# Phase 1 with x also stored by features, its mean subtracted by accumulating DMAs and no transposes of x

## The chip, the cores and the metric

The kernel runs on one core of a Trainium2 chip. The metric is the device time of one execution in microseconds; a time is the median of three runs.

## The reference

One transformer block over x of 2048 tokens by 640 features, all in float32:

```python
mod = (_silu(c) @ w_mod).reshape(c.shape[0], 6, 1, -1)
sa, ca, ga, sb, cb, gb = ...
h = _layernorm(x) * (1 + ca) + sa
x = x + ga * _A_ref(h, A_wqkv, A_w_phi, A_wo)
h = _layernorm(x) * (1 + cb) + sb
x = x + gb * _B_ref(h, B_w1, B_b1, B_w2, B_b2)
```

`_A_ref` projects h to q, k and v in 32 heads of 20 features, maps q and k of each head by a 20 x 20 matrix and two softmaxes (of the value and of its negative), sums the outer products of mapped k and v over all tokens, and divides what q reads from that sum by a normaliser. `_B_ref` is two dense layers with a squared ReLU between them. This case is about the first `_layernorm` and the three projections behind it.

## The kernel before

The 2048 tokens are 16 tiles of 128, taken in pairs j = 0 to 7. Phase 1 makes, for each pair, the normalised and modulated features `hT` with the features on the partitions: five chunks d of 128 features by 256 tokens, each as a rounded high part and a low remainder. TensorE multiplies them with the folded weights for k, v and q of each tile. A projection (`proj`, L402) is 30 matmuls, into two PSUM banks of 384 and 256 columns; there are four such banks (`pj`), so a third projection in a row needs the banks of the first.

How a pair's features are made (before):
- `load_x` (L221) loads 256 tokens by 640 features, tokens on the partitions, into one of two slots.
- `ln_parts` (L333) has three parts: ScalarE sums each row (L339) and GpSimd makes the negative mean (L340); ScalarE sums the squares of the centred row (L344) and GpSimd takes the root (L345, L346) and the product (L347); ScalarE scales and shifts the rows in place (L350).
- `t1` (L388) has TensorE turn chunks of 128 x 128 by the identity matrix into PSUM (`t_in`, L363, tile `ta`), and `t_out` has ScalarE apply the modulation (L374) and round to the high part (L375), and VectorE subtract for the low part (L89, `lo`).

The loop of phase 1 (L718) goes over tiles t = 2 to 13, with t = 2j and 2j + 1 for pair j. For each it has the k projection and its evacuation by ScalarE, the v projection, in even tiles the products of k and v of the two tiles before (`do_kv`, L450, tile `kvp`), the softmax of k (`spread` L433 on VectorE, `exps` L440 on ScalarE, `k_norm` L444 on VectorE), the q projection (tiles below 12; for 12 to 15 it comes later) and the softmax of q (`q_chain`, L471). The statistics of pair j + 1 are taken in the even tile of pair j, its first two chunks are turned at the end of that tile, the other three in the odd tile. For pair 7 the statistics already start in tile 10 and 11 and the chunks are spread over tiles 12 and 13. Between, the vectors of the modulation are accumulated by VectorE (`mod_mac`, L321) from rows of `w_mod` that SyncE loads into five slots, and `spread_row` (L329) writes the gate, a column of 5 elements on each of 128 partitions, to DRAM (L330) and fetches it back as a row spread over all partitions (L331), in tile 7's side work.

In this loop the order of TensorE is written out by hand. The orders of VectorE, ScalarE, GpSimd and SyncE are set by a scheduler with a time model of its own; each engine then works its list strictly in that order, and a waiting instruction holds up all behind it. SyncE issues nearly all DMAs; GpSimd issues one here, since it alone can accumulate or change types.

Of the kernel before, what the change touches and what calls it, by code (L numbers as in the profile page):

```python
# [21 lines left out]
NT = S // P  # L22
NC = D // P
# [9 lines left out]
EPS = 1e-5  # L33
POSTPONED = 4
WARM = 9
KEPT = NT - POSTPONED
W2_AT = 48
PLAIN = 2
DEALT = range(NT // 2)
# [13 lines left out]
def kernel(  # L53
    ctx: ExitStack,
    tc: tile.TileContext,
    x: bass.AP,
    wk5: bass.AP,
    wk1: bass.AP,
    wq5: bass.AP,
# [13 lines left out]
    nc = tc.nc  # L73
# [24 lines left out]
    dram = ctx.enter_context(tc.tile_pool(name="dram", bufs=1, space=bass.MemoryType.DRAM))  # L98
# [40 lines left out]
    def tp(name):  # L139
        return psA.tile([P, 512], F32, tag="tp", name=name)  # L140
# [6 lines left out]
    ET_ = mybir.EngineType  # L147
# [19 lines left out]
    mhalf = const.tile([P, 2], F32, name="mhalf")  # L167
# [3 lines left out]
    cols_a = const.tile([P, 10], F32, name="cols_a")  # L171
# [38 lines left out]
    raw, WM, RV, XB = {}, {}, {}, {}  # L210
# [8 lines left out]
                nc.sync.dma_start(raw[nm][2][:40, 1], w1)  # L219

    def load_x(j):  # L221
        XB[j] = tok2(f"x{j % 2}", f"xb{j}")
        nc.sync.dma_start(XB[j], x[256 * j : 256 * j + 256].rearrange("(i p) d -> p i d", p=P))

    def load_wm(d):
        WM[d] = flat(tok2(("k", "k", "q0", "q1", "w")[d], f"wm_{d}"))
# [106 lines left out]
    def ln_parts(xt, nm, spare=None):  # L333
        sm = small([P, 2], "sm", f"sm{nm}")
        sq = small([P, 2], "sq", f"sq{nm}")
        nb = small([P, 2], "nb", f"nb{nm}")
        for i in range(2):
            same = spare[i] if spare else xt[:, i] if nm[0] == "a" else row("s3", f"same{nm}_{i}")
            nc.scalar.activation(same, xt[:, i], AF.Identity, accum_out=sm[:, i : i + 1])  # L339
        nc.gpsimd.tensor_scalar(sm, sm, -1.0 / D, None, op0=ALU.mult)  # L340
        yield
        for i in range(2):
            junk = spare[i] if spare else row("s3", f"junk{nm}_{i}")
            nc.scalar.activation(junk, xt[:, i], AF.Square, bias=sm[:, i : i + 1], accum_out=sq[:, i : i + 1])  # L344
        nc.gpsimd.tensor_scalar(sq, sq, 1.0 / D, EPS, op0=ALU.mult, op1=ALU.add)  # L345
        nc.gpsimd.tensor_tensor(sq, sq, mhalf, op=ALU.pow)  # L346
# [4 lines left out]
        yield  # L351

    def layer_norm(xt, nm, spare=None):
        for _ in ln_parts(xt, nm, spare):
            pass
# [23 lines left out]
    HT, PK, EK, EQ, PQ = {}, {}, {}, {}, {}  # L379
# [3 lines left out]
    def newest(engine):  # L383
        return next(i for i in reversed(nc.cur_bb.bb.instructions) if i.engine == engine)

    DONE = []

    def t1(j, *ds, more=None):  # L388
        if 0 in ds:
            HT[j] = ht(f"hT{j}", j)  # L390
        p = tp(f"ta{j}_{ds[0]}")
# [72 lines left out]
    def q_out(t, p):  # L464
        if t < KEPT:
            PQ[t] = row("s2", f"q{t}")
# [4 lines left out]
    def q_chain(t, whole=True):  # L471
        if t < KEPT:
            EQ[t] = tok2(f"q{t % 2}", f"eq{t}")
# [53 lines left out]
    def wo_weights(*gs):  # L527
# [189 lines left out]
    pe.__enter__()  # L717
    for t in range(2, NT - 2):  # L718
        j, i = divmod(t, 2)
        if i == 0 and j < NT // 2 - 2:  # L720
            load_x(j + 2)
        PK[t] = row("s2", f"k{t}")
        to_sb(proj("k", t), PK[t])
        if t == NT - 4:
            t1(j + 1, 0, 1)
        norm = j + 1 if i == 0 and t < NT - 4 else j + 2 if t == NT - 5 else None
        if norm:
            if not i:
                parts = ln_parts(XB[norm], f"a{norm}")
# [12 lines left out]
        spread(PK[t], EK[t], f"k{t}")  # L742
        exps(EK[t])
        if norm and not i:
            next(parts)
        if i and t < NT - 4:
            t1(j + 1, 2, 3)
        with tc.issue_after(newest(ET_.DVE)):
            k_norm(EK[t], t)
        if t < NT - POSTPONED:  # L750
            do_q(t, (1, 3, lambda: t1(j + 1, 4, more=LAST_COL.get(t))) if i else None)
            if norm and i:
                with tc.issue_after(newest(ET_.Activation)), tc.issue_after(DONE[0]):
                    next(parts)
# [7 lines left out]
        if t == NT - 6:  # L762
            parts = ln_parts(XB[j + 2], f"a{j + 2}")
            with tc.issue_after(newest(ET_.Activation)):
                next(parts)
        SIDE[t]()
    pe.__exit__(None, None, None)
    behind.close()
# [96 lines left out]
    def load_e(t):  # L865
        if t >= KEPT:
            if t < NT:
# [320 lines left out]
    for j in range(NB):  # L1188
        nxt = j + 1 < NB
        b, c = 2 * j + 5, 2 * j + 6  # L1190
# [56 lines left out]
        if j == 7:  # L1247
            t2(0, 4)
            p = tp("gbt")[:NC, :P]
# [463 lines left out]
    by_hand.__exit__(None, None, None)  # L1713


_INS = ["x", "wk5", "wk1", "wq5", "wq1", "wv", "bd", "c", "w_ss", "w_mod", "wo", "w1", "b1", "w2", "b2"]


# [53 lines left out]
```

## Time and profile before

| | |
|---|---|
| time, median of 3 runs | 756.91 us (756.39 to 757.07) |
| span of the profiled execution | 754.9 us |
| TensorE busy | 749.6 us (99%) |
| VectorE busy | 607.5 us (80%) |
| ScalarE busy | 458.8 us (61%) |
| GpSimd busy | 170.4 us (23%) |
| share of TensorE in the chain that ended last | 86% |
| phase 1's loop, pairs 1 to 6 | 52.33 to 224.10 us |

The profiled execution is known by its span, from the first to the last instruction of the program; the runs' median is 2.0 us above it. In the profile's rows, PE is TensorE, PEld its weight loads, DVE VectorE, ACT ScalarE, POOL GpSimd and SP SyncE; a q behind a name means the engine's sequencer. L79 is the line of the helper that issues nearly all matmuls, so these are told apart by their tiles: pk, pv, pq for the three projections, kvp for the products of k and v. A row of a group gives the number of instructions, their busy time in us, the mean of one in ns, and the idle time of the engine just before them with what ended it. A row of a timeline gives the start and the length in us.

### The profile page before, as it was taken

The page shows a single profiled execution, that of the slowest core. Times are in us where ns is not written, and L with a number is a line of the kernel's source. Part 1 is how long each engine was busy: PE and PEld are TensorE (multiplying, and loading weights), DVE is VectorE, ACT ScalarE, POOL GpSimd, SP SyncE. Part 2 cuts the span into 40 slices and gives each one's busy share as a digit, 9 for nine tenths or more (in the row PEclk, how much of TensorE's full clock was granted, in tenths as well). Part 3 has the DMA queues.
Part 4 walks back from the last instruction along what each step waited for, and adds up shares of the span by engine and source line. Part 5 has one row for each costly group of instructions (what it writes and reads, how often), then busy time and mean ns, then how long its engine had stood idle before and what let it go on. Part 6 is the DMA issues. An engine that isn't in the chain of part 4 may idle for free.

```text
span 754.9 us, 15404 instructions
## 1 busy us (share of the span) xinstructions
PE 749.6 (99%) x5888; PEld 731.9 (97%) x5888; DVE 607.5 (80%) x1123; ACT 458.8 (61%) x1060; POOL 170.4 (23%) x365
## 2 busy tenths in 40 slices
PE   9999999999999999999999999999999999999998
PEld 9999999999999998998899999999999999999997
DVE  6598987988999899999755768787777776777766
ACT  5767666677863355556677757485574756647431
POOL 3001101011200237646303030132221313213110
PEclk9999999999999999999999999999999999999999
DMA  9811431342432264664777475897677767667461
GB/s 324 336 39 80 155 96 70 106 139 103 138 105 93 71 190 142 143 153 124 173 204 218 121 216 215 278 326 204 185 213 204 205 196 212 191 181 208 132 188 36
DMA packets 58931, 126.70 MB, mean 168 GB/s; under 512 B 7452, under 2 KB 16417, under 8 KB 58857
## 3 DMA queue, kind: packets, MB, share of 16 engines
q1 hardware_dynamic: 38706, 79.41, 32.1%
q0 software_dynamic: 17568, 41.00, 22.0%
q10 hardware_dynamic: 2583, 5.30, 1.9%
q8 instruction: 46, 0.75, 0.5%
q14 instruction: 28, 0.23, 0.1%
HBM read 100.94 MB, written 29.89 MB: 173 GB/s over the span
## 4 chain that ended last, share of the span: by engine, by line
PE 86%; DVE 11%; POOL 1%; issue 1%; ACT 0%; DVEq 0%; POOLq 0%
PE up L79 24%; PE acc L79 18%; PE pk L79 9%; PE pv L79 9%; PE pq L79 8%; PE acc3x L79 5%; PE pwo L79 3%; PE kvp L455 3%; DVE dn L883 3%; DVE scr L881 2%; DVE ezb L905 2%; PE foldk L281 1%; PE ta L363 1%; DVE ot L89 1%; POOL dn L889 1%; PE foldq L281 1%
## 5 line engine op out<-in xcount | busy, mean ns | idle before, releaser
L79 PE MATMUL up<-h,w 128*128 128x256 f32 x1640 | 204.4, 276 | 0.1
L79 PEld LDWEIGHTS up<-h,w 128*128 128x128 f32 x1640 | 196.4, 188 | 0.5 <-DVE h L89 0.3
L1321 ACT ACTIVATE ft<-up,b_t 128x256 f32<-128x256 f32 x104 | 48.9, 471 | 96.0 <-PE up L79 95.6
L79 PE MATMUL acc<-w,ra 128*128 128x384 f32 x452 | 97.5, 335 | 0.0
L79 PE MATMUL pwo<-wo,ot 128*128 128x256 f32 (+3 forms) x512 | 79.9, 311 | 0.4 <-DVE ot L89 0.4
L1322 DVE TENSOR_TENSOR ft<-ft 128x256 f32<-128x256 f32 x104 | 43.8, 421 | 43.0 <-ACT ft L1321 41.4
L79 PEld LDWEIGHTS pwo<-wo,ot 128*128 128x128 f32 (+1 forms) x512 | 74.3, 188 | 3.5 <-issue 2.7
L79 PE MATMUL pq<-wq,hT 128*128 128x384 f32 (+1 forms) x480 | 75.1, 311 | 0.0
L79 PEld LDWEIGHTS acc<-w,ra 128*128 128x128 f32 x452 | 72.7, 188 | 0.9 <-DVE ra L89 0.6
L79 PE MATMUL pk<-wk,hT 128*128 128x384 f32 (+1 forms) x480 | 72.7, 308 | 0.0
L79 PE MATMUL pv<-wv,hT 128*128 128x384 f32 (+1 forms) x480 | 71.6, 306 | 0.0
L79 PEld LDWEIGHTS pq<-wq,hT 128*128 128x128 f32 x480 | 71.0, 188 | 0.6 <-issue 0.2
L79 PEld LDWEIGHTS pk<-wk,hT 128*128 128x128 f32 x480 | 70.5, 188 | 0.4 <-issue 0.2
L79 PEld LDWEIGHTS pv<-wv,hT 128*128 128x128 f32 x480 | 70.0, 188 | 0.0
L89 DVE TENSOR_TENSOR ra<-ft,ra 128x384 fp32r<-128x384 f32 (+2 forms) x86 | 36.8, 449 | 32.7 <-ACT ra L1345 19.4
L1431 POOL DMA_DIRECT2D ring_a<-td_a x34 | 18.5, 544 | 117.1 <-PE acc L79 103.7
L1345 ACT ACTIVATE ra<-ft 128x384 fp32r<-128x384 f32 x48 | 25.2, 526 | 28.5 <-DVE ft L1322 22.4
L79 PE MATMUL acc3x<-w,ra 128*128 128x256 f32 x231 | 39.5, 278 | 0.0
L79 PEld LDWEIGHTS acc3x<-w,ra 128*128 128x128 f32 x231 | 37.2, 188 | 0.0
L1336 DVE TENSOR_TENSOR ft<-ft 128x128 f32<-128x128 f32 x136 | 33.4, 286 | 1.2
L446 DVE TENSOR_REDUCE sk<-ek 128x64 f32<-128x1280 f32 x16 | 23.7, 1483 | 12.4 <-ACT ek L441 10.8
L889 POOL TENSOR_TENSOR dn<-dn,rs_q 128x32 f32<-128x32 f32 x32 | 19.9, 622 | 59.0 <-DVE dn L883 58.7
(264 smaller groups left out, 1458.2 us busy)
## 6 DMA issues: line engine op xcount, KB each, us to landing
ring_c<-td_c POOLq DMA_DIRECT2D x34, 384.0 KB, 4.1
ring_a<-td_a POOLq DMA_DIRECT2D x34, 384.0 KB, 3.5
ring_b<-td_b POOLq DMA_DIRECT2D x34, 256.0 KB, 3.5
esp<-eq SPq DMA_DIRECT2D x12, 640.0 KB, 3.2
el<-esp SPq DMA_DIRECT2D x12, 640.0 KB, 4.4
rw<-in_w SPq DMA_DIRECT2D x23, 320.0 KB, 3.5
wm<-in_w_mod SPq DMA_DIRECT2D x20, 320.0 KB, 3.7
xb<-in_x SPq DMA_DIRECT2D x8, 640.0 KB, 4.0
```

The lines of the kernel that those rows point to most:

```text
L79: nc.tensor.matmul(o, a, b, start=first and i == 0, stop=last and i == len(terms) - 1, skip_group_check=skip,)
L89: (eng or nc.vector).tensor_tensor(out_lo, full, hi.bitcast(F32), op=ALU.subtract)
L281: nc.tensor.matmul(p[g // 3][:, (g % 3) * 120 : (g % 3) * 120 + n], r, bd_t[:120, g * 120 : g * 120 + n], start=True, stop=True,)
L446: nc.vector.tensor_reduce(s, heads(flat(e)), axis=AX.X, op=ALU.add)
L455: nc.tensor.matmul(kvp[g // 4][64 * c : 64 * c + 64, a : a + 2 * n].rearrange("p (s n) -> p s n", s=2), v[:, u], e[:, :, o : o + n], start ...
L883: nc.vector.tensor_reduce(dn.rearrange("p s h -> p (s h)"), heads(z), axis=AX.X, op=ALU.add)
L889: nc.gpsimd.tensor_tensor(dn[:, s], dn[:, s], rs[:, 1 - s], op=ALU.mult)
L1321: nc.scalar.activation(r, p, AF.Relu, bias=b1_t[:, f : f + 1])
L1322: nc.vector.tensor_tensor(r, r, r, op=ALU.mult)
L1336: nc.vector.tensor_tensor(t[:, o], t[:, a], t[:, b], op=op)
L1345: nc.scalar.activation(a[:, 0, :3], t[:, :3], AF.Copy)
L1431: nc.gpsimd.dma_start(RING[j, n, r], TD[n][r].bitcast(F32R))
```

## The change

The host stores x a second time as `x_t`: for each pair a block of 128 partitions by 5 chunks by 256 tokens, features on the partitions. From pair 2 on (TURNED = 2):

- `load_xt` loads that block into the slot `x1`; the block by tokens takes the slot `x0` alone, and is used for the statistics only.
- `row_parts` replaces `ln_parts`: the sums and the means as before, then `put_row` writes the negative means (two elements on each of 128 partitions) to DRAM as a row of 256, and `centre` has GpSimd issue two accumulating DMAs that add this row to every partition of the features' block. Then the squares, the root, a second `put_row`, and `get_row`, which fetches the row of factors spread over all partitions.
- `t1` has VectorE multiply the block by that row (new line 431), and `t_out` reads the product from SBUF in place of PSUM. TensorE turns no x from pair 2 on; it still turns the pieces of the modulation.
- All pairs follow one scheme: statistics of pair j + 1 in the even tile of pair j. That holds for pair 7 too, whose features are now made in pair 6 alone. `load_x` for pair j + 2 comes behind the statistics of pair j + 1.

```diff
+TURNED = 2
...
+    def put_row(j, k, col):
+        nc.sync.dma_start(LR[j][k].rearrange("(i p) -> p i", p=P), col)
+
+    def centre(j):
+        for a, b in ((0, 2), (2, NC)):
+            nc.gpsimd.dma_start(XT[j][:, a:b], LR[j][0][None, None, :].to_broadcast([P, b - a, 256]), accum_op=ALU.add)
+
+    def get_row(j):
+        RB[j] = row("s3", f"rb{j}")[:, :256]
+        nc.sync.dma_start(RB[j], LR[j][1][None, :].to_broadcast([P, 256]))
...
+    def row_parts(j):
...
+        for i in range(2):
+            nc.scalar.activation(xt[:, i], xt[:, i], AF.Identity, accum_out=sm[:, i : i + 1])
+        nc.gpsimd.tensor_scalar(sm, sm, -1.0 / D, None, op0=ALU.mult)
+        put_row(j, 0, sm)
+        centre(j)
+        yield
+        for i in range(2):
+            nc.scalar.activation(xt[:, i], xt[:, i], AF.Square, bias=sm[:, i : i + 1], accum_out=sq[:, i : i + 1])
...
+        nc.gpsimd.tensor_tensor(sq, sq, mhalf, op=ALU.pow)
+        put_row(j, 1, sq)
+        get_row(j)
+        yield
...
+        if j >= TURNED:
+            u = XT[j][:, ds[0] : ds[-1] + 1]
+            nc.vector.tensor_tensor(u, u, RB[j][:, None, :].to_broadcast([P, len(ds), 256]), op=ALU.mult)
...
+            for d in ds:
+                t_out(cols_a, HT[j], d, f"a{j}", XT[j][:, d], XT[j][:, d])
...
-        12: lambda: t1(NT // 2 - 1, 2, 3),
...
-        if i == 0 and j < NT // 2 - 2:
-            load_x(j + 2)
+        if i == 0:
+            load_xt(j + 1)
...
-        if norm and not i:
+        if i == 0:
             next(parts)
+            if j < NT // 2 - 2:
+                load_x(j + 2)
...
-        if i and t < NT - 4:
+        if i:
             t1(j + 1, 2, 3)
...
-        if i == 0 and t < NT - 4:
+        if i == 0:
             t1(j + 1, 0, 1)
```

VectorE's order in pair 2, before, behind the softmax's sums of k of tile 4: the two maxima of q (`mxq`), then the low parts of the first two chunks of the next pair (`hT`).

```order
L448 TENSOR_TENSOR ek_1263<-ek_1263,sk_1273 128x1280
L435 TENSOR_REDUCE mxq_1313<-q_1309 128x32
L436 TENSOR_REDUCE mxq_1313<-q_1309 128x32
L89 TENSOR_TENSOR hT_1322<-hfa_0_1328,hT_1322 128x256
L89 TENSOR_TENSOR hT_1322<-hfa_1_1332,hT_1322 128x256
L297 SCALAR_TENSOR_TENSOR wm_1_1336<-wm_1_1336,cs,wm_0_1152 128x640
L438 TENSOR_TENSOR eq_1312<-q_1309,mxq_1313 128x640 x2
```

The same place with the change; `xt` is the block by features, `rb` the fetched row of factors.

```order
L484 TENSOR_REDUCE mxq_1306<-q_1302 128x32
L485 TENSOR_REDUCE mxq_1306<-q_1302 128x32
L496 RECIPROCAL sk_1266<-sk_1266 128x64
L487 TENSOR_TENSOR eq_1305<-q_1302,mxq_1306 128x640
L431 TENSOR_TENSOR xt_1144<-xt_1144,rb_1254 128x512 x2
L431 TENSOR_TENSOR xt_1144<-xt_1144,rb_1254 128x256
L487 TENSOR_TENSOR eq_1305<-q_1302,mxq_1306 128x640
L497 TENSOR_TENSOR ek_1258<-ek_1258,sk_1266 128x1280
L484 TENSOR_REDUCE mxk_1401<-k_1329 128x32
L485 TENSOR_REDUCE mxk_1401<-k_1329 128x32
L91 TENSOR_TENSOR hT_1315<-xt_1144,hT_1315 128x256 x2
```

All five chunks are multiplied at one place, between the two halves of the softmax's differences of q (`eq`), and the low parts come behind the normalising of k and the maxima of the next tile's k.

SyncE's order at the start of pair 4, before: the load of x for a later pair, the gate's column and its fetch, the store of a tile of exponentials (`esp`).

```order
L223 DMA xb_1849<-in_x 128x2x640
L330 DMA gate_186<-gate_a 128x5x1
L331 DMA ga_b<-gate_186 128x640
L485 DMA esp_195<-eq_1834 128x1280
L316 DMA wm_4_2037<-in_w_mod 128x640
L496 DMA rwo_2191<-in_wo 60x640 x2
```

The same place with the change; `lr` are the two rows of statistics in DRAM.

```order
L231 DMA xt_1817<-in_x_t 128x1280
L350 DMA gate_186<-gate_a 128x5x1
L351 DMA ga_b<-gate_186 128x640
L235 DMA lr_0_1819<-sma_1856 128x2x1
L225 DMA xb_1936<-in_x 128x2x640
L534 DMA esp_195<-eq_1802 128x1280
L235 DMA lr_1_1820<-sqa_1857 128x2x1
L336 DMA wm_4_2003<-in_w_mod 128x640
L545 DMA rwo_2149<-in_wo 60x640 x2
L243 DMA rb_1934<-lr_1_1820 128x256
```

Both rows of statistics and the fetch of the factors stand behind the gate's column and its fetch.

GpSimd's order around the statistics of pair 3's features, with the change.

```order
L379 TENSOR_SCALAR sma_1183<-sma_1183 128x2
L239 DMA xt_1144<-lr_0_1146 128x2x256
L239 DMA xt_1144<-lr_0_1146 128x3x256
L385 TENSOR_SCALAR sqa_1184<-sqa_1184 128x2
L386 TENSOR_TENSOR sqa_1184<-sqa_1184,mhalf 128x2
```

The two accumulating DMAs, which wait for the first row in DRAM, stand ahead of the root that the second row needs.

More of the change, by code (lines that the diff above doesn't have):

```diff
@@ L56 @@
     x: bass.AP,
+    x_t: bass.AP,
     wk5: bass.AP,
@@ L221, in load_x, with load_xt @@
     def load_x(j):
-        XB[j] = tok2(f"x{j % 2}", f"xb{j}")
+        XB[j] = tok2(f"x{j % 2}" if j < TURNED else "x0", f"xb{j}")
         nc.sync.dma_start(XB[j], x[256 * j : 256 * j + 256].rearrange("(i p) d -> p i d", p=P))
+    XT, LR, RB = {}, {}, {}
+    def load_xt(j):
+        XT[j] = flat(tok2("x1", f"xt{j}")).rearrange("p (d n) -> p d n", d=NC)
+        nc.sync.dma_start(XT[j], x_t[j * P : (j + 1) * P].rearrange("p (d n) -> p d n", d=NC))
+        LR[j] = [dram.tile([256], F32, name=f"lr{j}_{k}") for k in range(2)]
+    def put_row(j, k, col):
[6 more added lines that the diff above has]
+        nc.sync.dma_start(RB[j], LR[j][1][None, :].to_broadcast([P, 256]))
     def load_wm(d):
@@ L351, in ln_parts @@
         yield
+    def row_parts(j):
+        xt = XB[j]
+        sm = small([P, 2], "sm", f"sma{j}")
+        sq = small([P, 2], "sq", f"sqa{j}")
+        for i in range(2):
[6 more added lines that the diff above has]
+            nc.scalar.activation(xt[:, i], xt[:, i], AF.Square, bias=sm[:, i : i + 1], accum_out=sq[:, i : i + 1])
+        nc.gpsimd.tensor_scalar(sq, sq, 1.0 / D, EPS, op0=ALU.mult, op1=ALU.add)
+        nc.gpsimd.tensor_tensor(sq, sq, mhalf, op=ALU.pow)
+        put_row(j, 1, sq)
+        get_row(j)
+        yield
     def layer_norm(xt, nm, spare=None):
@@ L719 @@
         j, i = divmod(t, 2)
-        if i == 0 and j < NT // 2 - 2:
-            load_x(j + 2)
+        if i == 0:
+            load_xt(j + 1)
         PK[t] = row("s2", f"k{t}")
         to_sb(proj("k", t), PK[t])
[L724 to L729, printed above, removed]
+        if i == 0:
+            parts = row_parts(j + 1)
             with tc.issue_after(newest(ET_.Activation)):
@@ L743 @@
         exps(EK[t])
-        if norm and not i:
-            next(parts)
-        if i and t < NT - 4:
+        if i:
             t1(j + 1, 2, 3)
@@ L759 @@
                 q_chain(t)
-        if i == 0 and t < NT - 4:
+        if i == 0:
             t1(j + 1, 0, 1)
[L762 to L765, printed above, removed]
         SIDE[t]()
```

12 lines of the change are left out of this document (8 added, 4 removed).

## The prediction

> **What bounds the kernel now.** I read the shares of the chain that ended last, then a table of stretches cut at the starts of the pairs of phase 1, then TensorE's timeline of one such pair.
>
> ```profile
> by line: PE up L79 24.5%; PE acc L79 18.0%; PE pk L79 9.2%; PE pv L79 9.1%; PE pq L79 7.8%; PE acc3x L79 5.0%; PE pwo L79 3.5%; PE kvp L455 2.6%; DVE dn L883 2.6%; DVE scr L881 2.5%; DVE ezb L905 2.2%; PE foldk L281 1.0%; PE ta L363 0.9%; D
> ```
> ```profile
> core 0: us, PE busy (x) PEld busy (x) DVE busy (x) ACT busy (x) POOL busy (x), PEclk, DMA share, GB/s
> 52.33:82.14 29.81, 29.81 (x237) 29.59 (x235) 26.84 (x34) 20.98 (x48) 2.31 (x6) 1.00 0.24 86
> 82.14:111.95 29.81, 29.81 (x236) 29.59 (x235) 26.82 (x35) 19.56 (x44) 2.84 (x4) 1.00 0.36 116
> 111.95:142.32 30.37, 30.37 (x241) 30.15 (x240) 26.18 (x35) 19.33 (x45) 2.83 (x4) 1.00 0.30 99
> 142.32:172.65 30.33, 30.33 (x242) 30.11 (x241) 26.88 (x34) 21.05 (x48) 2.88 (x6) 1.00 0.35 108
> 172.65:202.97 30.32, 30.32 (x242) 30.10 (x241) 27.69 (x35) 24.47 (x58) 7.07 (x11) 1.00 0.32 108
> 202.97:224.10 21.13, 21.13 (x176) 20.88 (x175) 20.53 (x30) 12.92 (x30) 0.00 (x0) 1.00 0.37 124
> ```
> ```profile
> 82.14 4.46 PE L79 MATMUL pk<-wk,hT 128*128 128x384 f32 x30
> 86.44 4.46 PE L79 MATMUL pv<-wv,hT 128*128 128x384 f32 x30
> 90.83 2.54 PE L455 MATMUL kvp<-ek,vt 128*64 128x120 f32 x44
> 93.30 4.64 PE L79 MATMUL pq<-wq,hT 128*128 128x384 f32 x30
> 97.78 0.60 PE L363 MATMUL ta<-ident,xb 128*128 128x128 f32 x4
> ```
>
> The rows of the table are pairs j = 1 to 6. TensorE is busy from end to end of each, at full clock, so what is removed from it there shortens the kernel, as long as nothing else becomes late. VectorE is the near rival: 26.8 of 29.8 us, and 20.5 of 21.1 in pair 6. Below, times within a pair count from its first key matmul (82.14 is 0 for pair 2).
>
> **What the change removes.** The 60 transposes of x (ta L363) hold 0.9% of the chain: 0.009 x 754.9 = 6.8 us, 1.1 per pair. A plain pair falls from 29.8 to about 28.7. ScalarE loses the two scalings L350, and has slack anyway.
>
> **What it adds on VectorE.** One multiplication of 1280 elements per pair, in three pieces.
>
> ```profile
> L448 DVE TENSOR_TENSOR ek<-ek,sk 128x1280 f32<-128x1280 f32 x10 | 14.8, 1485 | 0.1
> L446 DVE TENSOR_REDUCE sk<-ek 128x64 f32<-128x1280 f32 x10 | 14.9, 1485 | 11.1 <-ACT ek L441 10.6 <-ACT ek L442 0.2
> L438 DVE TENSOR_TENSOR eq<-q,mxq 128x640 f32<-128x640 f32 x22 | 17.0, 811 | 0.0
> L435 DVE TENSOR_REDUCE mxk<-k 128x32 f32<-128x640 f32 x10 | 8.1, 811 | 0.0
> L89 DVE TENSOR_TENSOR hT<-hfa,hT 128x256 fp32r<-128x256 f32 x24 | 9.3, 419 | 1.5 <-ACT hT L375 1.5
> ```
>
> By L448 that is 1.5 us, so VectorE has 28.3 us of work for a pair of 28.7: alone it would just fit, since the 10.6 us in which it waited for the exponentials of k mostly followed the two removed scalings. But it has no room left to wait.
>
> **What it adds as a wait.** The statistics now reach the features through DRAM: sums, a row of 256 means written in 4-byte pieces, the accumulating DMA, then the root, a second such row, and a broadcast fetch. In the order of the change GpSimd has the accumulating DMAs ahead of the root, so the two writes follow one another. VectorE stands in order behind the fetch. The nearest rows are these: sums of pair 2, GpSimd's small steps, the one column write of before and a row write, and small loads.
>
> ```profile
> 86.64 0.39 ACT L431 ACTIVATE k<-pk 128x256 f32<-128x256 f32 x1 [0.42 <-PE pk L79]
> 88.27 0.19 ACT L339 ACTIVATION_READ_ACCUMULATOR xb<-xb 128x1 f32 x1
> ```
> ```profile
> L346 POOL TENSOR_TENSOR sqa<-sqa,mhalf 128x2 f32<-128x2 f32 x6 | 5.5, 924 | 0.5
> L345 POOL TENSOR_SCALAR sqa<-sqa 128x2 f32<-128x2 f32 x6 | 2.5, 413 | 14.3 <-ACT junka L344 14.3
> L340 POOL TENSOR_SCALAR sma<-sma 128x2 f32<-128x2 f32 x6 | 1.8, 294 | 120.5 <-ACT xb L339 120.5
> L508 POOL DMA_DIRECT2D wo<-wo x1 | 0.8, 789 | 34.0 <-DVE wo L89 34.0
> ```
> ```profile
> 144.26 0.38 SPq L330 DMA_DIRECT2D gate<-gate_a  x1
> 154.62 0.34 SPq L331 DMA_DIRECT2D ga_b<-gate  x1
> ```
> ```profile
> 388.53 0.28 SPq L1252 DMA_DIRECT2D gate<-gate_r  x1
> 389.73 0.32 SPq L1253 DMA_DIRECT2D gb_b<-gate  x1
> ```
> ```profile
> rwo<-in_wo SPq DMA_DIRECT2D x10, 150.0 KB, 2.5
> ga_b<-gate SPq DMA_DIRECT2D x1, 320.0 KB, 3.9
> rawv<-in_wv SPq DMA_DIRECT2D x5, 320.0 KB, 11.5
> ```
>
> The fetch at 154.62 reads what the write at 144.26 puts down, and is SyncE's next DMA: the write of 640 single elements held the queue 10.4 us. Its twin, the same 2.5 KB as five rows of 512 bytes, let its fetch go after 1.2 us. So the price lies in the number of pieces. I take 1.2 as the part without pieces and scale the rest: W = 1.2 + 9.2 x 256/640 = 4.9 us for a row of 256. Ends: 1.2, and 10.4 if the price does not fall with the count.
>
> The Trainium skill ("DMA: Bandwidth & Descriptors", "Anatomy of one DMA") gives a DMA a fixed cost of about 2.0 us plus its bytes, which would make W 2.0. The 10.4 us of this trace do not agree with it for 2.5 KB, and I go by the trace; what W = 2.0 would do is the first rival.
>
> The chain of a plain pair: sums read at 88.27 + 0.19, so 6.3; L340 0.3 and the issue, 6.7; W, 11.6; two accumulating DMAs issued by GpSimd at 0.8 each (L508), 13.2; L345 and L346, 14.5; W, 19.5; the fetch of 128 KB at 2.5 us (nearest row 150 KB; 3.9 as upper end), 22.0. Before, VectorE would be at this place after the two maxima of q, when pq ends at 97.78 (15.6): some 17.5 to 19. So it waits 3 to 4.5 us per pair. The accumulating DMA of 640 KB is hidden if it lands within 8.8 us; 11.5 us, the slowest load above, would add 2.7. ScalarE too stands in order behind the multiplication, with the second half of the next tile's k to evacuate behind that; that has a few us of room.
>
> From the multiplication to the last hT subtraction VectorE has in pair 2: 1.5, one half of eq 0.8, ek 1.5, two maxima 1.6, five subtractions 2.1, one step for the modulation 0.9, two halves of ek 1.6, one sum of eq 1.5: 11.5, or 11.0 with the pipelined overlap of about 0.08 each that the timeline's starts show. So the last features are there at 33.0; the next pair's first projection needs them 2.0 us after its start (4.3 us x 384/640 for its first bank, x 12/15 matmuls), so it starts in effect at 31.0 instead of 29.8: +1.2. In pairs 1 and 3 fewer steps stand between (10.3, 10.5): +0.5 and, against 30.4, +0.2. Sum for three pairs: +1.9.
>
> **Pair 4, behind the gate.** Here SyncE's order has the gate column's write and fetch ahead of the first row. The gate's sum follows the late features, so the write goes at about 4.2, the fetch 10.4 later, and the row at 15.0 instead of 6.7. Statistics land at 30.3. ScalarE's evacuation of tile 9's k waits behind them, to about 34.5 (multiply 1.3, scalings and copies of four chunks); the q projection of tile 9 needs that PSUM bank, so TensorE, which would have been there at 24.3, stands 10 us; with pq 4.3 the pair ends at 38.8 against 30.3: +8.5. VectorE has then 12.7 us of delayed work until tile 9's keys are normalised, 13.1 into pair 5, where kvp wants them at 8.7: 4.4 of waiting, less the gain: +2.9.
>
> **Pair 6.** Before, its successor's features were prepared from tile 11 on; now all of it lies in the short pair 6. Features of pair 7 begin at 22.0; first chunk at 24.2, five chunks at ScalarE's pace by 27.5, so the key projection starts at 25.5 in effect against 21.1: +4.4, and 0.5 for tile 13's steps pushed behind.
>
> Sum: 1.9 + 8.5 + 2.9 + 4.9 = +18.2. The span is 754.9, and the median of the runs, 756.9, is 2.0 above it for what lies around; I forecast 756.9 + 18.2 = 775. Each 1 us in W moves up to 2 us in six pairs, 12 in all; with W at 6 and the fetch at 3.9, or the accumulation late by 2.7, it is 795 to 805.
>
> **Rivals.**
> (a) Small writes are cheap here (chance 0.17): W 1.2, by the row write. The fetch lands at 14.6, ahead of VectorE; all 6.8 us are gained. Pair 4 keeps the gate in front: row at 15.0, statistics at 22.9, the bank free at 27.1 instead of 24.3: some +2.4. 756.9 - 6.8 + 2.4 = 752.5. For it: 5 rows took 1.2 us. Against: the 10.4 us. The skill's fixed 2.0 us puts the fetch at 16.2 and gives the same 752.5.
> (b) The write's time does not fall with the count (0.08): W 10.4, chain 11 us longer in six pairs: 775 + 66 = 841.
> (c) W near 3 (0.13): the fetch lands at 18.2, about when VectorE comes; pairs 1 to 3 gain 3.5, pair 4 loses 4.5, pairs 5 and 6 1.6: 759.5. A little less W turns its sign: slower 0.08, same 0.03, faster 0.02.
> My own case (W 4 to 6) has 0.62.
>
> Slower: 0.62 + 0.08 + 0.08 = 0.78; same 0.03; faster 0.17 + 0.02 = 0.19, the bound being 0.2% (1.5 us), about what a measurement tells here. The range runs from (a), 752, to the upper end of my case, 805; outside it stay (b) and a tenth.
>
> **What would show it.** Right: the fetch of the first row issued some 5 us after its write; VectorE idle before L431 for 3 us and more, longest in pair 4; TensorE's first gaps in phase 1, at pq of tile 9, at kvp and at the first pk of pair 7. Wrong: second-row fetches issued within 2 us of their writes, no gap on TensorE, phase 1 shorter by 1.1 us a pair; or equal gaps of 11 us in every pair.

## The result and the profile after

| | before | change |
|---|---|---|
| time, median | 756.73 us (756.16 to 757.07, 5 runs) | 887.64 us (886.85 to 890.24, 5 runs) |
| span of the profiled execution | 754.9 us | 885.2 us |
| TensorE busy | 749.6 us (99%) | 764.1 us (86%) |
| clock granted to TensorE, mean of the span | 1.00 in phase 1 | 0.93, in phase 1 0.78 to 0.84 |

The ratio is 1.1743 (95% interval 1.1730 to 1.1756): slower by 131 us, where 775 us (752 to 805) was forecast. The sign was right, the size was not, and the range did not hold it.

The chain that ended last, by engine and by line, of the profile after. The entries `lr<-sqa`, `lr<-sma`, `xt<-lr` and `rb<-lr` are the new transfers:

```profile
PE 60%; DVE 13%; DMA 11%; issue 11%; ACT 3%; POOL 1%; SPq 0%; POOLq 0%; DVEq 0%; ACTq 0%
PE up L81 21%; PE acc L81 15%; PE pwo L81 5%; PE acc3x L81 4%; PE pq L81 4%; DMA lr<-sqa 4%; PE pk L81 4%; DMA lr<-sma 3%; DMA xt<-lr 2%; PE pv L81 2%; PE te L962 1%; DMA rb<-lr 1%; DVE ezb L942 1%; DVE dn L920 1%; DVE scr L918 1%
```

The table of stretches, cut at the first key matmul of pairs 1 to 6 and at the end of pair 6, as it was shown of before:

```profile
core 0: us, PE busy (x) PEld busy (x) DVE busy (x) ACT busy (x) POOL busy (x), PEclk, DMA share, GB/s
52.20:98.09 45.89, 30.58 (x227) 29.75 (x225) 22.86 (x30) 16.65 (x41) 4.41 (x7) 0.82 0.44 61
98.09:144.71 46.62, 32.99 (x224) 32.00 (x225) 27.09 (x37) 17.28 (x43) 3.78 (x5) 0.83 0.53 105
144.71:195.53 50.82, 32.84 (x229) 31.52 (x230) 28.92 (x39) 19.08 (x47) 4.28 (x5) 0.84 0.43 87
195.53:254.17 58.64, 33.10 (x231) 32.56 (x230) 30.20 (x42) 18.64 (x46) 4.92 (x7) 0.78 0.51 105
254.17:305.33 51.16, 31.86 (x231) 31.44 (x230) 27.46 (x38) 20.33 (x47) 5.43 (x8) 0.80 0.48 82
305.33:350.18 44.85, 21.93 (x166) 21.30 (x165) 23.50 (x31) 14.76 (x33) 3.71 (x5) 0.79 0.53 98
```

Every pair is longer, by 16 to 28 us: together 298.0 us against 171.8, which is 126 of the 130 us between the spans. TensorE, busy from end to end before, works 30.6 of the first 45.9 us, and at 0.82 of its clock. What it waits for in phase 1 (engine, tile, what ended the wait; total, times, longest):

```profile
PE pq L81 <- ACT k L480: 86.7, 5, 23.3
PE pk L81 <- ACT k L480: 17.5, 1, 17.5
PE kvp L504 <- DVE ek L497: 7.9, 3, 5.4
```

TensorE stands before the queries of the odd tile (in pair 6 before the first keys of pair 7) because ScalarE has not evacuated the keys, and ScalarE stands behind VectorE's multiplication. The next views follow that back in pair 1. ScalarE's part first: it waits 21.16 us for the multiplication, then scales two chunks (L412), then evacuates the keys (L480).

```profile
92.29 1.09 ACT L412 ACTIVATE xt<-xt,cols_a 128x256 f32<-128x256 f32 x2 [21.16 <-DVE xt L431]
93.29 0.36 ACT L480 ACTIVATE k<-pk 128x256 f32<-128x256 f32 x1
```

SyncE's queue, GpSimd and VectorE, each a start and a length:

```profile
58.84 0.38 SPq L235 DMA_DIRECT2D lr<-sma  x1
78.70 0.37 SPq L235 DMA_DIRECT2D lr<-sqa  x1
87.61 0.33 SPq L243 DMA_DIRECT2D rb<-lr  x1
```
```profile
69.22 1.43 POOL L239 DMA_DIRECT2D xt<-lr  x1 [9.84 <-DMA lr<-sma]
75.92 1.30 POOL L239 DMA_DIRECT2D xt<-lr  x1 [5.26 <-issue]
77.31 0.29 POOL L924 TENSOR_SCALAR dd<-dd 128x32 f32<-128x32 f32 x1
77.68 0.19 POOL L385 TENSOR_SCALAR sqa<-sqa 128x2 f32<-128x2 f32 x1
77.95 0.72 POOL L386 TENSOR_TENSOR sqa<-sqa,mhalf 128x2 f32<-128x2 f32 x1
```
```profile
91.57 1.63 DVE L431 TENSOR_TENSOR xt<-xt,rb 128x512 f32<-128x512 f32 x3 [21.56 <-issue]
```

The chain has the order that the prediction gave it; its links are longer. From the pair's start at 52.20, in us:

| link | predicted | measured |
|---|---|---|
| sums, L379, issue of the first row | 6.7 | 6.6 |
| first row of 256, to GpSimd's next instruction | 4.9 | 10.4 |
| two accumulating DMAs issued | 1.6 | 8.1 |
| to the issue of the second row | 1.3 | 1.4 |
| second row, to the issue of the fetch | 4.9 | 8.9 |
| fetch, to the multiplication | 2.5 | 4.0 |
| multiplication starts at | 22.0 | 39.4 |

Two rows show their wait as "issue", for which the profile names no semaphore. The multiplication's 21.56 us end when the fetch has landed, 3.9 us after its issue; both accumulating DMAs had landed by 83.3. The second accumulating DMA waits 5.26 us, and is issued at 75.92, just when the first has landed (75.66).

TensorE in the same pair; the third row is the start of pair 2:

```profile
76.44 2.76 PE L81 MATMUL pq<-wq,hT 128*128 128x384 f32 x15
93.70 3.57 PE L81 MATMUL pq<-wq,hT 128*128 128x256 f32 x15 [14.50 <-ACT k L480]
98.09 2.29 PE L81 MATMUL pk<-wk,hT 128*128 128x384 f32 x6 [0.81 <-ACT vt L475]
```

The last row's six matmuls take 2.29 us, 0.38 each; the fifteen of the first row, of the same width, took 0.18 each. The stretch around the gap shows why (the third number from the end is the granted clock, 0.50):

```profile
81.80:102.30 20.50, 7.78 (x28) 7.49 (x29) 10.73 (x18) 8.26 (x21) 0.00 (x0) 0.50 0.18 43
```

So the clock fell to half 2.6 us after the last matmul and came back 8.6 us after work had begun again, with short waits between. By the trace's clock records, the six long gaps differ in this: the fall came 2.6 to 5.3 us after the last matmul, the return 4.7 to 8.6 us after the first new one. In the six pairs TensorE is busy 183.3 us, where 171.8 less the 6.8 of transposes is 165.0: some 18.3 us, an estimate, are the price of matmuls at half clock. The Trainium skill ("TensorE: Matmul & The Clock Gate", "Part 1: The HAM clock gate") has the clock halve after an idle window of some 3.4 us and return after as long a busy one. The trace agrees with the half; the times scatter around that figure for the fall and lie above it for the return.

The other transfers also grew. Issues of phase 1's DMAs (KB each, median us to landing), first of before, then of after:

```profile
esp<-eq SPq DMA_DIRECT2D x12, 640.0 KB, 3.2
xb<-in_x SPq DMA_DIRECT2D x8, 640.0 KB, 4.0
```
```profile
esp<-eq SPq DMA_DIRECT2D x12, 640.0 KB, 10.7
xb<-in_x SPq DMA_DIRECT2D x8, 640.0 KB, 10.9
xt<-lr POOLq DMA_DIRECT2D x6, 384.0 KB, 8.4
xt<-lr POOLq DMA_DIRECT2D x6, 256.0 KB, 7.0
rb<-lr SPq DMA_DIRECT2D x6, 128.0 KB, 3.9
```

The medians of `esp` and `xb` in the change rest on few DMAs: the profile tells the landing of three of the twelve stores (11.2, 2.9 and 10.7 us) and of two of the loads (10.6 and 11.3). The store of 2.9 us was issued at 97.63, when no row was on its way. So it is the transfers beside a row that are slow, not all.

Theory after this: the rows of 4-byte pieces cost some 9 us whatever their count, and the accumulating DMAs hold GpSimd, so the multiplication starts 17 us late and everything behind it follows. Rivals: the accumulating DMAs are slow by themselves; VectorE has no room for the multiplications, so that the pairs would be long without any late statistics; ScalarE's order does it.

### The profile page after: what moved, and what is told of

Its sections match the earlier page's. It is cut to its first block, busy times and chain, and to the rows that moved or that the text cites. A ratio compares the mean times of both kernels' runs of the same rounds, so it can differ in the third digit from the quotient of the medians.

```text
span 885.2 us, 15380 instructions
## 1 busy us (share of the span) xinstructions
PE 764.1 (86%) x5828; PEld 742.7 (84%) x5828; DVE 615.8 (70%) x1141; ACT 448.3 (51%) x1048; POOL 179.3 (20%) x371
## 4 chain that ended last, share of the span: by engine, by line
PE 60%; DVE 13%; DMA 11%; issue 11%; ACT 3%; POOL 1%; SPq 0%; POOLq 0%; DVEq 0%; ACTq 0%
PE up L81 21%; PE acc L81 15%; PE pwo L81 5%; PE acc3x L81 4%; PE pq L81 4%; DMA lr<-sqa 4%; PE pk L81 4%; DMA lr<-sma 3%; DMA xt<-lr 2%; PE pv L81 2%; PE te L962 1%; DMA rb<-lr 1%; DVE ezb L942 1%; DVE dn L920 1%; DVE scr L918 1%
## 5 line engine op out<-in xcount | busy, mean ns | idle before, releaser
L81 PE MATMUL pq<-wq,hT 128*128 128x384 f32 (+1 forms) x480 | 84.4, 337 | 86.7 <-ACT k L480 86.7
L81 PEld LDWEIGHTS pq<-wq,hT 128*128 128x128 f32 x480 | 79.9, 211 | 88.7 <-ACT k L480 88.1
L431 DVE TENSOR_TENSOR xt<-xt,rb 128x512 f32<-128x512 f32 (+1 forms) x18 | 9.9, 599 | 135.4 <-DMA rb<-lr 68.3
L81 PE MATMUL pk<-wk,hT 128*128 128x384 f32 (+1 forms) x480 | 79.3, 325 | 19.5 <-ACT k L480 17.5
L81 PEld LDWEIGHTS pk<-wk,hT 128*128 128x128 f32 x480 | 76.6, 201 | 21.5 <-ACT k L480 17.7
L412 ACT ACTIVATE xt<-xt,cols_a 128x256 f32<-128x256 f32 x30 | 16.2, 590 | 140.7 <-DVE xt L431 140.7
L1382 ACT ACTIVATE ra<-ft 128x384 fp32r<-128x384 f32 x48 | 25.2, 525 | 28.5 <-DVE ft L1359 22.4
L239 POOL DMA_DIRECT2D xt<-lr x12 | 15.7, 1305 | 97.9 <-issue 46.0
## 6 DMA issues: line engine op xcount, KB each, us to landing
esp<-eq SPq DMA_DIRECT2D x12, 640.0 KB, 10.7
xb<-in_x SPq DMA_DIRECT2D x8, 640.0 KB, 10.9
```

What stands on the lines that cost most here:

```text
L81: nc.tensor.matmul(o, a, b, start=first and i == 0, stop=last and i == len(terms) - 1, skip_group_check=skip,)
L239: nc.gpsimd.dma_start(XT[j][:, a:b], LR[j][0][None, None, :].to_broadcast([P, b - a, 256]), accum_op=ALU.add)
L412: nc.scalar.activation(hf, p[:, :256], AF.Identity, bias=cols[:, d : d + 1], scale=cols[:, 5 + d : 6 + d])
L431: nc.vector.tensor_tensor(u, u, RB[j][:, None, :].to_broadcast([P, len(ds), 256]), op=ALU.mult)
L1382: nc.scalar.activation(a[:, 0, :3], t[:, :3], AF.Copy)
```

## The experiments

Times are medians, each beside 756.3 to 756.7 us of the kernel before on the same chip.

### More space for GpSimd's descriptors

Descriptors are the lists of what a DMA is to move; this setting is the space for those of GpSimd's DMAs.

```diff
-    nc = bacc.Bacc("TRN2", target_bir_lowering=False, num_devices=1, dynamic_dma_scratch_size=1024)
+    nc = bacc.Bacc("TRN2", target_bir_lowering=False, num_devices=1, dynamic_dma_scratch_size=2048)
```

> The changed kernel with twice the space for GpSimd's DMA descriptors (2048 in place of 1024), nothing else. Theory: in every pair the second accumulating DMA was issued only when the first had landed (75.66, then 75.92 us), for want of descriptor space, and the root and the second row stood behind it. Then the second is issued some 1.5 us behind the first, each of six chains is 5 to 6.5 us shorter, and the time falls from 887.6 to 845 to 860. Rival: the second waits for the first's data or for the queue itself: gap and time stay, 885 to 890.

Measured: 879.97 us, ratio 1.163 (1.156 to 1.170), between the two ranges: the pause went as the theory had it, the time did not. GpSimd, then SyncE's queue, in pair 1 (which starts at 52.04):

```profile
69.87 2.76 POOL L239 DMA_DIRECT2D xt<-lr  x2 [10.65 <-DMA lr<-sma]
```
```profile
74.11 0.37 SPq L235 DMA_DIRECT2D lr<-sqa  x1
85.59 0.33 SPq L243 DMA_DIRECT2D rb<-lr  x1
```

The pause is gone, both accumulating DMAs are issued in 2.76 us: the descriptors' space was its cause. But the second row, now written beside both accumulations, takes 11.5 us in place of 8.9, and 7.7 us in all are won. The space was a link of the chain. In pair 1 its 5.3 us bring the multiplication only 1.8 us forward (37.6 us into the pair in place of 39.4), the rest came back in the next links.

### Rows as two pieces of 512 bytes

The row is written from two partitions of 128 elements, which GpSimd makes as a product of the identity and the statistics; the numbers written are not the statistics.

```diff
-nc.sync.dma_start(LR[j][k].rearrange("(i p) -> p i", p=P), col)
...
+r = RB[j][:2, 256 + P * k : 384 + P * k]
+nc.gpsimd.tensor_tensor(r, ident[:2], col[:2, 0:1].to_broadcast([2, P]), op=ALU.mult)
+nc.sync.dma_start(LR[j][k].rearrange("(i p) -> i p", p=P), r)
```

> The changed kernel with both rows of statistics written as two pieces of 512 bytes from a small product on GpSimd, in place of 256 pieces of 4 bytes; the rows then hold products with the identity, not the statistics, so the features are wrong. Theory: the pieces are the price, 7.4 to 10.9 us a row; the writes take 1.2 to 2 us, each chain is 15 us shorter, TensorE's half clock mostly goes with its gaps, and the time is 775 to 800. Rival: the rows are slow because they stand behind large transfers in the queues: writes stay above 6 us and the time above 860.

Measured: 815.50 us, ratio 1.078 (1.075 to 1.081), 15 us above the theory's range and far below the rival's. The same 1 KB in two pieces is worth 72 us. In pair 1 GpSimd goes on 1.7 us after the first row's issue in place of 10.4. GpSimd's second accumulating DMA, then SyncE's queue:

```profile
68.25 1.31 POOL L243 DMA_DIRECT2D xt<-lr  x1 [5.49 <-issue]
```
```profile
71.12 0.24 SPq L239 DMA_DIRECT2D lr<-rb  x1
75.01 0.32 SPq L247 DMA_DIRECT2D rb<-lr  x1
```

Left in the chain are 5.5 us of waiting for descriptor space, 3.9 for the second row beside the accumulation, and the fetch.

### Root, second row and fetch ahead of the accumulating DMAs

> The changed kernel with the root, the second row and its fetch ahead of the accumulating DMAs on GpSimd. Theory: the two row writes then overlap, the fetch lands near 26 us into a pair, and the multiplication waits for the second accumulating DMA instead, near 31 in place of 39: 835 to 855. If two rows in flight together only slow each other down: 870 to 890. If the accumulation was never near the end of the chain (lands by 26): 810 to 830.

Measured: 864.66 us, ratio 1.143 (1.134 to 1.152), between two of the ranges. SyncE's queue in pair 1 (starts near 52):

```profile
58.60 0.38 SPq L235 DMA_DIRECT2D lr<-sma  x1
62.25 0.37 SPq L235 DMA_DIRECT2D lr<-sqa  x1
77.67 0.33 SPq L243 DMA_DIRECT2D rb<-lr  x1
```

The root is ready before the first row has landed, as meant. But the second row takes 15.4 us. Its fetch goes 8.4 us after the first row has landed (69.3 by the trace's landing records), as if it had begun only then; the first accumulating DMA runs beside it, so the two causes are not told apart. In pair 1 the last multiplications wait for the second accumulating DMA, until 33.6 us into the pair, which the theory had near 31. GpSimd's order was worth 23 us, less than its place in the chain suggests.

### Small writes that nobody waits for, in the kernel before

Ten DMAs of a few elements behind the side work of tiles 2 to 11, of six kinds. They tell what a row's price depends on.

> The kernel before, with a small store to DRAM behind the q sums of each of tiles 1 to 10 that nobody waits for: 256 pieces of 4 bytes side by side, 128 of them, 256 of them 512 bytes apart, 128 pieces of 16 bytes side by side, 256 of 4 bytes 64 bytes apart, two rows of 512 bytes, and the first four once more. If the price goes by the number of pieces: 128 take half of 256, spacing does nothing. If pieces that share a line of memory wait for one another: 256 spaced ones land in 1.5 to 3 us, 128 side by side take as long as 256, and 16-byte pieces are cheaper. If the price is of the queue alone, the two rows of 512 bytes take as long. Time 757 to 762.

The landings that the profile tells, four of the ten (min, median, max):

```profile
DMA to landing us min/median/max: 2.1/8.7/11.4
```

By kind, the last of the sixteen DMA engines to land, from the trace's landing records. The sixth kind, two rows of 512 bytes, is not in the table, since the profile does not tell its landing; in the run with such rows above, GpSimd went on 1.7 us after the issue.

| pieces | us |
|---|---|
| 256 of 4 bytes, neighbours | 8.3, 11.4 |
| 128 of 4 bytes, neighbours | 9.2, 8.6 |
| 256 of 4 bytes, 64 bytes apart | 2.1 |
| 256 of 4 bytes, 512 bytes apart | 3.2, 1.6 |
| 128 of 16 bytes, neighbours | 1.9, 1.9 |

Half the pieces cost as much, and the same 256 pieces spread out cost a fifth. The count does not set the price; 4-byte pieces that lie beside each other do. That the memory takes such neighbours one after another is argued from this, not shown. The Trainium skill ("DMA: Bandwidth & Descriptors", "Anatomy of one DMA") gives a fixed cost of about 2.0 us whatever the size, fitted on DMAs that GpSimd issues, where these are SyncE's: the spread and the 16-byte pieces lie at 1.6 to 3.2 us, near it, the neighbours do not, and the measurement decides. The kernel took 762.98 us with these ten writes, in a single run: writes that nobody waits for are not free; a load of x behind one of 128 neighbours landed in 10 to 11 us, where 4 is usual.

### No statistics at all

Row writes, accumulating DMAs and fetch left out; VectorE multiplies by ones, so nothing is normalised.

> Leaves out what carries the statistics (both row writes, the accumulating DMAs, the fetch); VectorE multiplies by ones instead, so the output is not normalised. Sums, squares and root are still computed. It prices the removal by itself, with VectorE's added multiplications. If all the loss comes from the wait for statistics: no gaps on TensorE in phase 1, its clock back at 1.0 there, and the 6.8 us of transposes gained: 748 to 752 us. Rival: VectorE, with 28.3 us of work in a pair of 28.7, is already too full, and the multiplications by themselves make the pairs longer: 757 to 775 us, TensorE waiting for hT or for eq.

Measured: 772.30 us, ratio 1.021 (1.020 to 1.023), in the rival's range. But TensorE waits neither for `hT` nor for `eq`; it waits for the normalised keys:

```profile
PE kvp L500 <- DVE ek L493: 14.7, 3, 7.6
```

In pair 2 the next pair's three multiplications stand ahead of the normalising of the keys, as in the change, and here sums of q, a step of the modulation and the differences of the next keys stand between them as well. So this run mixes VectorE's load with its order, and prices neither.

### Rows of 512 bytes, root first and more space

The three edits together.

> Rows written as two pieces of 512 bytes (from a product of the identity and the statistics, so the numbers written are not the statistics), root, second row and fetch ahead of the accumulating DMAs, and descriptor space of 2048 instead of 1024. If the write's pieces, GpSimd's order and the space were the whole of it, what is left per pair is a row at 7, root 11, row 2 at 14, fetch at 18, accumulation behind that at about 20 to 22: TensorE waits less than 5 us a pair: 757 to 785 us. If the accumulating DMAs are slow for their own sake (6 to 8 us here, whatever stands beside them) the features wait for them: 785 to 815 us.

Measured: 794.77 us, ratio 1.050 (1.049 to 1.052): the second theory's range. VectorE's multiplications in pair 1, the first chunks and the rest:

```profile
70.17 0.69 DVE L436 TENSOR_TENSOR xt<-xt,rb 128x512 f32<-128x512 f32 x1 [3.27 <-DMA rb<-lr]
75.48 1.03 DVE L436 TENSOR_TENSOR xt<-xt,rb 128x512 f32<-128x512 f32 x2 [4.62 <-DMA xt<-lr]
```

With the root in time, the second accumulating DMA is what comes last, at 23 us into the pair. The accumulations matter for their own sake.

### Statistics spread by TensorE

TensorE transposes each statistic's column read with stride zero, which leaves it as a row on every partition; ScalarE copies it from PSUM, GpSimd adds the mean. In the first run VectorE multiplies, in the second GpSimd.

```diff
+nc.tensor.transpose(p[:, a : a + P], col[:, i : i + 1].to_broadcast([P, P]), ident)
...
+nc.gpsimd.tensor_tensor(u, u, RB[j][:, 0:1].to_broadcast([P, b - a, 256]), op=ALU.add)
```

> No DRAM at all: TensorE transposes each statistic's column read with stride zero, which gives it on every partition as a row (4 transposes a pair in place of 10), ScalarE copies it from PSUM, GpSimd adds the negative mean, VectorE multiplies. If only the way of the statistics cost time: 60 - 24 = 36 transposes fewer, 4.1 us, so 751 to 755 us, if GpSimd's additions end before VectorE comes (about 17.5 us into a pair). If GpSimd takes over 5 us for the 1280 elements, VectorE and ScalarE wait behind it and the gaps come back smaller: 757 to 785 us.

> As the run before, but GpSimd also multiplies, so VectorE has the work of the kernel before. If VectorE's 1.5 us a pair matter: faster than the run before by 1 us or more (750 to 753 us). If GpSimd is the slow one (two passes of 1280 elements, a share of the memory port with VectorE): slower than the run before, 757 to 790 us, with TensorE waiting for hT.

Measured: 765.16 us, ratio 1.012 (1.010 to 1.013), and 759.67 us, 1.005 (1.003 to 1.006). Without DRAM nearly all of the loss is gone, the gain does not come, and the multiplications on VectorE cost 5.5 us, with what the scheduler's order changes with them. The first run is in its second range, but not for the reason given there: TensorE waits 6.0 us for normalised keys, not for features. The second run beats the first, which its second theory excluded, and misses the 750 to 753 of the other. Its pairs 1 and 2 take 28.9 us each, 0.9 less than before; at the start of pair 6 it is 2.2 us ahead, and loses that in pair 6 and at the start of pair 7, where TensorE waits for the features.

### The root alone

The mean is left out of the features: no first row, no accumulating DMA. First the root goes by the change's row of 4-byte pieces, then by two pieces of 512 bytes, then so with GpSimd multiplying in VectorE's place.

> Leaves the mean out: no first row, no accumulating DMAs, so the mean is not subtracted; the root goes as in the change, by a row of 4-byte pieces and a fetch. With a landing of 9 and a fetch of 3.9 the fetch is there 10.9 + 9 + 3.9 = 24 us into a pair. By the prediction's own chain behind the fetch (last features 11 us after it, 2 us of slack in the next pair) the total is 775 + 6 x 2 = 787 us, so 775 to 800. Rival: ScalarE's evacuations behind the multiplication hold TensorE in every pair, not in pair 4 alone, and its clock falls to half after each: 800 to 840 us.

> As the run before, with the root's row as two pieces of 512 bytes from a product with the identity (the numbers written are not the root): the fetch is there 10.9 + 0.5 + 1.1 + 3.9 = 16.4 us into a pair, before VectorE comes (17.5). By the prediction's first rival: 752 to 756 us. Rival: VectorE has no room for 1.5 us more a pair (the run without statistics lost 15.6 us to before): 760 to 775 us, TensorE waiting at kvp for the normalised keys.

> As the root alone by rows of 512 bytes (769.4 us, nothing late, 13 us over before), with the multiplications on GpSimd instead of VectorE; mean left out and root's numbers replaced as there. If VectorE's 1.5 us a pair were the 13 us: keys normalised in time, 752 to 757 us. If the order of VectorE's other work is at fault (normalised keys behind other steps) it stays: 763 to 770 us.

Measured: 808.69 us, ratio 1.069 (1.068 to 1.071); 769.41 us, 1.018 (1.016 to 1.020); 762.20 us, 1.008 (1.006 to 1.009). The first run's queue and multiplication in pair 1, which begins at 51.48 and ends at 84.95:

```profile
61.77 0.37 SPq L235 DMA_DIRECT2D lr<-sqa  x1
70.30 0.33 SPq L243 DMA_DIRECT2D rb<-lr  x1
```
```profile
75.24 1.63 DVE L429 TENSOR_TENSOR xt<-xt,rb 128x512 f32<-128x512 f32 x3 [9.80 <-DMA rb<-lr]
```

The multiplication starts 23.8 us into the pair, the expectation had 24; the pair lasts 33.5 us, the prediction's chain has 24 + 11 - 2 = 33. But the two meet by luck. TensorE does not wait for the features here, it waits for ScalarE, which stands behind the multiplication with the queries and the keys:

```profile
PE pv L81 <- ACT q L478: 2.7, 1, 2.7
PE pq L81 <- ACT k L478: 1.6, 1, 1.6
```

That is the rival's mechanism, and 808.69 lies in the rival's range. In later pairs the multiplication is later (26.0 and 27.6, and 36.0 behind the gate), TensorE waits for ScalarE's evacuations and for normalised keys, and its clock is 0.84 to 0.95 in pairs 3 to 6. The second run is its rival's answer too, in range and in the wait: 11.8 us at kvp for normalised keys. The third lies between its two ranges. Stretches of the third run, pairs 1, 4 and 6:

```profile
52.11:80.65 28.54, 28.54 (x227) 28.32 (x225) 26.09 (x33) 18.75 (x46) 5.75 (x9) 1.00 0.35 127
...
138.26:172.59 34.33, 31.05 (x232) 30.51 (x230) 26.30 (x33) 17.30 (x42) 5.94 (x9) 0.95 0.41 140
...
201.95:227.48 25.53, 21.80 (x167) 21.35 (x165) 22.26 (x28) 15.44 (x37) 7.29 (x7) 0.93 0.51 165
```

Plain pairs gain 1.3 us. Pair 4 loses 4.0, with the root's row still behind the gate's write, and pair 6 4.4, of which TensorE waits 3.7 for normalised keys.

### Pair 7 by tokens, and the place of four transposes

From the run at 759.67 us: pair 7 prepared as in the kernel before; then also the statistics' transposes 9 in place of 3 matmuls into the query projection in pairs 3 to 5; then also pair 7's first transposes between the two products of keys and values.

> Statistics spread by TensorE, GpSimd adds and multiplies, as in the run at 759.7; pair 7 by tokens as in the kernel before (its transposes too, 10 more, 1.1 us). That run stood 2.2 us ahead of before at the start of pair 6 and lost 5.2 us from there. If pair 7's preparation inside the short pair 6 is what lost them: 754 to 756 us, faster than before. If VectorE and ScalarE are late there for another reason: 758 to 761 us.

> As the run before, but in the three pairs with modulation transposes the statistics' four transposes stand 9 instead of 3 matmuls into the q projection, since TensorE waited there 1.2 us in all for the PSUM bank (st behind ScalarE's copy of mt). If that wait is given back: 0.5 to 1.2 us faster than the run before. If GpSimd's two passes end that much later and the features are late: no faster, or slower by up to 2 us.

> As the later spread (756.5 us), whose pair 6 began 4.2 us ahead of before and gave 3.5 of it back waiting for pair 7's tokens (0.8), for the keys of tile 11 (1.15) and in between: pair 7's first transposes stand between the two key-value products, the next after tile 13's keys. If these waits were all: 753 to 755 us, faster than before. If ScalarE and VectorE are behind in pair 6 whatever the order: 756 to 759 us.

Measured: 763.61 us, ratio 1.010 (1.008 to 1.011); 756.51 us, 1.0003 (0.9995 to 1.0012); 756.35 us, 0.9996 (0.9987 to 1.0005). The first missed both its ranges, the second won 7.1 us where 1.2 was the most expected. Of the 7.1, pairs 3 to 5 gave 2.4 and pair 6 5.0. TensorE's waits of these two in pair 6 name most of the second part:

```profile
PE kvp L514 <- DVE ek L507: 5.5, 1, 5.5
```
```profile
PE kvp L514 <- DVE ek L507: 1.1, 1, 1.1
```

With six matmuls' difference on TensorE the normalising of the keys has another place in VectorE's order: from behind the sums of q and the differences of the next keys (it starts at 215.74) to ahead of both (211.07). In the last run TensorE never waits in pairs 1 to 5, which take 146.9 us against 150.6 before, and pair 6 takes 24.1 against 21.1: it gives 3 of the 3.8 us back, 1.6 of it waiting for keys. That is the second of its two theories. No version tried beats the kernel before.

The pairs side by side, in us:

| pair | before | change | root by 4-byte row | root by 512-byte rows | and GpSimd multiplies | last version |
|---|---|---|---|---|---|---|
| 1 | 29.8 | 45.9 | 33.5 | 28.5 | 28.5 | 28.9 |
| 2 | 29.8 | 46.6 | 34.7 | 28.5 | 28.5 | 28.9 |
| 3 | 30.4 | 50.8 | 38.3 | 29.6 | 29.1 | 29.5 |
| 4 | 30.3 | 58.6 | 46.9 | 36.1 | 34.3 | 29.8 |
| 5 | 30.3 | 51.2 | 36.0 | 31.8 | 29.4 | 29.7 |
| 6 | 21.1 | 44.9 | 32.0 | 28.7 | 25.5 | 24.1 |

From the column "and GpSimd multiplies" leftwards, the medians give a ladder: 762.2 with the root alone and nothing on VectorE; 7.2 more for its multiplications, with the orders that the scheduler makes of them; 39.3 more when the root's row is of 4-byte pieces; 78.9 more for the mean's row, its accumulating DMAs and the root behind them. The other way down, 512-byte rows alone took 72 us off the change, so rows and accumulations are not simply additive.

## Why the prediction was wrong, step by step

**The step that failed: W = 1.2 + 9.2 x 256/640 = 4.9.** It scaled the gate's 10.4 us by the number of pieces. The count does not set the price (128 pieces cost what 256 do); in the change the rows landed in 7.4 to 10.9 us. The two rows are 5.5 + 4.0 = 9.5 of the 17.4 us by which pair 1's multiplication is late. The upper end, 10.4, was in the text and was right, but as a rival with a chance of 0.08, outside the range. The upper end of 805 does not come out of its own terms either: W at 6 with the fetch at 3.9 gives 797, the accumulation late by 2.7 gives 791. The fault was to draw a line through two points that differ in two things: the pieces' number and whether they are 4-byte neighbours.

**"Two accumulating DMAs issued by GpSimd at 0.8 each."** 8.1 us in pair 1 in place of 1.6: each takes 1.3 to 1.4 to issue, and the second waits some 5 us until the first has landed. That GpSimd could run out of descriptor space was not considered; the run with twice the space showed it. Landing late, the accumulations also bound the run with everything else cured, at 23 us into the pair. The prediction bounded that by 8.8 us and 2.7 above it, and held it hidden.

**The fetch** took 4.0, not 2.5: the upper end of 3.9 given for it was the right row.

**The chain's form was right up to the multiplication, and behind it in part.** The forecast had the plain pairs end with the last features, 11 us after the fetch, and ScalarE's evacuation hold TensorE in pair 4 alone, since ScalarE had a few us of room elsewhere. At 39.4 that room is used up in all six pairs: of the 114.7 us in which TensorE stands, 104.2 are for ScalarE's keys and 1.1 for features. Pair 1 by the forecast's rule would last 39.4 + 11 - 2 = 48.4; it lasts 45.9, because TensorE goes on 2.1 us after the multiplication starts and has half a query projection left. So the rule of 6 us in all for 1 us of landing, which gives 775 + 6 x 17.4 = 879 against 888, comes close with luck: whatever stands behind the multiplication moves with it. The 33 and 33.5 of the run with the root alone are luck in the same way.

**What was not in the sum:** the clock. Gaps of 13 to 23 us leave TensorE at half clock, some 18.3 us of longer matmuls. They end up inside a pair that waits anyway, so they may not be added whole.

**Gain term, 1.1 us a pair:** right; plain pairs take 28.5 us in the runs with the root in time, where 28.7 was forecast.

**VectorE "would just fit":** right in the plain pairs, where it makes no difference who multiplies (28.5 both). It costs 7.2 us in all, in pairs 3 to 6; whether by load or by order is not shown.

**Pair 4:** the row went out 14.3 us into the pair, 15.0 was forecast. The pair was 28.3 us longer, not 8.5, for the same reasons as the others. **Pair 5:** 2.9 was forecast from keys that come 13.1 us into it, at kvp; TensorE does not wait at kvp there. The 13.1 has no working: the 12.7 us of delayed work, counted from the evacuation at 34.5, end at 47.2, which is 8.4 into pair 5 and in time for the 8.7. **Pair 6:** 4.9 was forecast for features of pair 7 that come late; in the run with GpSimd multiplying it cost 4.4, but by luck: the wait was 3.7 us for normalised keys, and 0.3 for features at the start of pair 7. That pair 7 by tokens still left 3 us there is not explained in full.

**The rivals.** Cheap writes (a): with rows of 512 bytes the change stands at 815.5, not 752.5, so this rival would have failed too, on the accumulations and GpSimd's wait for descriptor space. Rival (b), a price without count, had the right W; its 841 is short by the accumulations' wait. The test "equal gaps of 11 us in every pair" pointed the right way: 14.5 us in pair 1.

## What to carry to other kernels

When a price is known from one row, find what it depends on before scaling it; here a run with a few kinds of small write would have replaced the scaling, and rival (b) would have been the forecast, a loss of 84 us, still 47 short. A value that goes through DRAM inside a loop has a chain of its own: write it down from issue to issue, and give each link its slow end when several such transfers are in flight together. A gain of 1 us per stage on a full engine lasts only if every other engine keeps its order; the scheduler's next order can take 7 us for a change of six matmuls.

## What the hardware showed beside

- Neighbouring 4-byte pieces cost 8 to 11 us for 128 or 256 of them; spread 64 bytes apart 2.1, as 16-byte pieces 1.9. With two such writes in flight they took 11 and 15 us, the second beside an accumulating DMA.
- Bystanders pay: beside the rows a store `esp` took 10.7 or 11.2 us, 3.2 before, and the loads `xb` 10.6 or 11.3, 4.0 before.
- With 1024 of descriptor space the second accumulating DMA waits for the first's landing; with 2048 it does not.
- A transpose of a column read with stride zero spreads it over all partitions: two of them stand in the traces of those runs at 0.38 to 0.40 us.
- GpSimd's additions of 128 x 512 and 128 x 768 elements took 1.42 and 1.99 us, its multiplications 2.13 and 2.33 (means of the run at 759.67 us).
